# An mLSTM cell with its result laid out features-on-partitions: array halves and quarters, block transpose, shuffle, and a trip through memory

## Chip, cores, metric

One core of a Trainium2 chip. The metric is device time of one execution in microseconds (us), lower is better. A kernel's time is the median of its executions, which agree within 1%. "Granted clock" is the share of TensorE's full clock that the profile records as granted. Engines: PE is TensorE (PEld its weight load), DVE VectorE, ACT ScalarE, POOL GpSimd, SP SyncE, whose only work here is to issue DMAs, in order (in the changed kernel's queue below, the loads of xT at 383.03 us stand behind an output store that goes out at 381.40).

## The reference, cut to what matters

Batch 4, 8 heads, 768 tokens, head dimension 40; then a SwiGLU block, 320 to 1536 to 320, all fp32.

```
for t in range(S):                       # per batch and head
    m_new = max(f[t] + m, i[t])
    C = exp(f[t] + m - m_new) * C + exp(i[t] - m_new) * outer(v[t], k[t])
    n = exp(f[t] + m - m_new) * n + exp(i[t] - m_new) * k[t]
    y[t] = sigmoid(o[t]) * (C @ q[t]) / max(abs(n . q[t]), 1)
x = y as (tokens, heads * 40)
out = (silu(x @ w_gate) * (x @ w_val)) @ w_out
```

With these inputs n·q, computed by the reference, stays under 0.274 in size, so the clamp gives 1 throughout and the division changes nothing.

## The kernel before

The cell is computed in chunks of 128 tokens ("units"), six per batch element, 24 in all. Three units make a group of 384 tokens; there are eight groups. For each group PE first runs the *generator* (gate and value products over 12 slices of the 1536 features, with the next group's scores between them), then the *projection*, nine parts of 2.155 us, into which the cell of the next group is set. The next generator needs the next group's result, transposed, as `xT`. Each unit's weights `w` are made on DVE, POOL and ACT from a load of M, a running maximum of the gates that is computed at the start and kept in memory.

```
def attend(u):                                   # the cell of one unit
    inter[:, heads] = qT @ C                     # 4 full-array products
    y = inter * e_T                              # DVE
    add = k.T @ v_w;  new C = add + kept         # PE, POOL, DVE
    for h in range(H):                           # tokens on partitions: 41 streamed columns
        nc.tensor.matmul(intra[:, h, :], lhsT=un["w"][:, h, :], rhs=un["v"][:, h, :], start=True, stop=True)
    y = y + intra                                # DVE
    den = 1 / max(abs(y[:, :, D:]), 1)           # DVE, 8 elements per token
    x = o * y * den                              # POOL, DVE; x_sb has one buffer
    xx = x, each half doubled                    # POOL

def seam(u):                                     # features onto partitions, on PE
    for kc in range(NKC):
        nc.tensor.transpose(tp[:, kc, :], units[u]["x"][:, kc], ident)      # tp_x
    nc.scalar.copy(xts[g][...], tp)              # xT

# ... cut: order inside one projection of nine parts, n = -1 .. 8
follow = {-1: [(attend, nxt[0])], 1: [(attend, nxt[1])], 3: [(attend, nxt[2])],
          4: [(seam, nxt[0])], 5: [(seam, nxt[1])], 7: [(seam, nxt[2])]}
for n, u in zip((4, 5, 6), after):
    follow.setdefault(n, []).append((turn, u))   # k, q transposes of the group after
```

All DMAs are issued by SyncE. While the first group runs, DVE also converts the block's weights (`raw`) into their working form, 18 pieces.

Of the kernel before, what the change touches and what calls it, by code (L numbers as in the profile page):

```python
# [9 lines left out]
F32 = mybir.dt.float32  # L10
U32 = mybir.dt.uint32
AF = mybir.ActivationFunctionType
# [5 lines left out]
L = 128  # L18
# [4 lines left out]
def kernel(  # L23
# [22 lines left out]

    nc = tc.nc
# [5 lines left out]
    D1 = D + 1  # L53
# [7 lines left out]
    assert NB * L == S and NFC * 128 == DF and TW <= 512 and D <= DP and BH <= 128 and NKC * HP == DM  # L61
# [17 lines left out]
    NRK, NRQ, NRO = 2 * GC, GC + 1, GC + 1  # L79
    k_ring = [const.tile([128, H, DP], F32, name=f"k{r}") for r in range(NRK)]  # L80
    q_ring = [const.tile([128, H, DP], F32, name=f"q{r}") for r in range(NRQ)]
    v_ring = [const.tile([128, H, D1], F32, name=f"v{r}") for r in range(NRK)]
    for r in range(NRK):
        nc.vector.memset(k_ring[r][:, :, D:], 0.0)
        nc.gpsimd.memset(v_ring[r][:, :, D:], 1.0)
    for r in range(NRQ):
        nc.vector.memset(q_ring[r][:, :, D:], 0.0)

# [6 lines left out]
    def tokens(a, u):  # L95
        b, c = divmod(u, NB)
        return a[b, :, ts(c, L), :].rearrange("h p d -> p h d")

    def load(u):
        un = units[u] = {"k": k_ring[u % NRK], "q": q_ring[u % NRQ], "v": v_ring[u % NRK]}  # L100
        nc.sync.dma_start(out=un["k"][:, :, 0:D], in_=tokens(k, u))
        nc.sync.dma_start(out=un["q"][:, :, 0:D], in_=tokens(q, u))
        nc.sync.dma_start(out=un["v"][:, :, 0:D], in_=tokens(v, u))

    def load_o(u):
        un = units[u]
        un["o"] = work.tile([128, H, D], F32, name="o_sb", bufs=NRO)
        nc.sync.dma_start(out=un["o"], in_=tokens(o_gate, u))
        nc.scalar.activation(un["o"], un["o"], AF.Sigmoid)
# [14 lines left out]
    nc.vector.reduce_sum(pair, idb.rearrange("p (a two) -> p a two", two=2), axis=AX.X)  # L124
    half = const.tile([BH, 2], F32)
    nc.vector.reduce_sum(half, idb.rearrange("p (a two) -> p two a", two=2), axis=AX.X)
# [3 lines left out]
    C_ring = [const.tile([128, PR, 2, D1], F32, name=f"C{r}") for r in range(2)]  # L130
# [7 lines left out]
    def flat(t):  # L138
        return t.rearrange("p c t -> p (c t)")
# [10 lines left out]
    M_dram = tc.dram_tile([BH, S], F32, name="M_dram")  # L150
    nc.sync.dma_start(out=M_dram, in_=flat(M_sb))
# [4 lines left out]
    nc.scalar.activation(e_sb, e_sb, AF.Exp)  # L156


    g_T = const.tile([128, NB, BH], F32)
    e_T = const.tile([128, NB, BH], F32)  # L160
    for dst, src, c0 in ((g_T, g_sb, 0), (e_T, e_sb, 1)):
        tp = psum.tile([128, NB, BH], F32, name="tp_g", tag="cell")
        for c in range(c0, NB):
            nc.tensor.transpose(tp[:, c, :], src[:, c - c0, :], idb)
        nc.vector.tensor_copy(dst[:, c0:, :], tp[:, c0:, :])
# [55 lines left out]
    def weigh(u):  # L221

        b, c = divmod(u, NB)
        un = units[u]
        w = un["w"] = work.tile([128, H, L], F32, name="w_sb", bufs=2 * GC - 1)
        src = M_dram[b * H:(b + 1) * H, ts(c, L)].unsqueeze(0).to_broadcast([128, H, L])
        nc.sync.dma_start(out=w, in_=src)
        gb = g_T[:, c, b * H:(b + 1) * H].unsqueeze(2).to_broadcast([128, H, L])
        nc.vector.tensor_tensor(w, gb, w, op=ALU.subtract)  # L229
        nc.gpsimd.affine_select(w, w, compare_op=ALU.is_ge, fill=NEG, base=0, pattern=[[0, H], [1, L]],  # L230
                                channel_multiplier=-1)
        nc.scalar.activation(w, w, AF.Exp)  # L232
        if c + 1 < NB:
            un["v_w"] = work.tile([128, H, D1], F32, name="v_w", bufs=GC + 1)
            nc.gpsimd.tensor_tensor(un["v_w"], un["v"], w[:, :, L - 1:L].to_broadcast([128, H, D1]), op=ALU.mult)  # L235
# [10 lines left out]
    def scores(u):  # L246
        un = units[u]
        sps = [psum.tile([128, PR, L], F32, name="sp", tag="cell") for _ in range(2)]
        for j in range(PR):
            for two in range(2):  # L250
                r = slice(two * DP, two * DP + DP)
                nc.tensor.matmul(sps[two][:, j, :], lhsT=un["kT"][r, j, :], rhs=un["qT"][r, j, :], start=True, stop=True)  # L252
        w2 = un["w"].rearrange("p (j two) t -> p two j t", two=2)
        for two in range(2):
            nc.vector.tensor_tensor(w2[:, two], sps[two], w2[:, two], op=ALU.mult)  # L255

    def attend(u):
        b, c = divmod(u, NB)
        un = units[u]
        y = un["y"] = work.tile([128, H, D1], F32, name="y_sb")  # L260
        old = state.get("C")
        if c > 0:
            inter = psum.tile([128, H, D1], F32, name="inter", tag="cell")
            for j in range(PR):
                nc.tensor.matmul(inter[:, 2 * j:2 * j + 2, :].rearrange("p h d -> p (h d)"), lhsT=un["qT"][:, j, :],  # L265
                                 rhs=old[:, j].rearrange("p a d -> p (a d)"), start=True, stop=True)
            nc.vector.tensor_tensor(y, inter, e_T[:, c, b * H:(b + 1) * H].unsqueeze(2).to_broadcast([128, H, D1]),
                                    op=ALU.mult)
        if c + 1 < NB:
            add = psum.tile([128, PR, 2, D1], F32, name="add", tag="cell")  # L270
            for j in range(PR):
                nc.tensor.matmul(add[:, j].rearrange("p a d -> p (a d)"),  # L272
                                 lhsT=un["k"][:, 2 * j:2 * j + 2, :].rearrange("p h d -> p (h d)"),
                                 rhs=un["v_w"][:, 2 * j:2 * j + 2, :].rearrange("p h d -> p (h d)"),
                                 start=True, stop=True)
            new = C_ring[u % 2]
            if c > 0:
                d = dec[:, c - 1, b * PR:(b + 1) * PR].unsqueeze(2).unsqueeze(3).to_broadcast([128, PR, 2, D1])
                kept = work.tile([128, PR, 2, D1], F32, name="kept", bufs=1)
                nc.gpsimd.tensor_tensor(kept, old, d, op=ALU.mult)  # L280
            for two in range(2):
                r = slice(two * DP, two * DP + DP)
                if c > 0:
                    nc.vector.tensor_tensor(new[r, :, two], add[r, :, two], kept[r, :, two], op=ALU.add)  # L284
                else:
                    nc.vector.tensor_copy(new[r, :, two], add[r, :, two])
            state["C"] = new
        intra = psum.tile([128, H, D1], F32, name="intra", tag="cell")
        for h in range(H):
            nc.tensor.matmul(intra[:, h, :], lhsT=un["w"][:, h, :], rhs=un["v"][:, h, :],  # L290
                             start=True, stop=True)
        if c > 0:
            nc.vector.tensor_tensor(y, y, intra, op=ALU.add)  # L293
        else:
            nc.vector.tensor_copy(y, intra)
        den = work.tile([128, H, 1], F32, name="den")
        nc.vector.scalar_tensor_tensor(den, in0=y[:, :, D:], scalar=-1.0, in1=y[:, :, D:], op0=ALU.mult, op1=ALU.max)
        nc.vector.tensor_scalar(den, den, scalar1=1.0, scalar2=None, op0=ALU.max)
        nc.vector.reciprocal(den, den)
        x = work.tile([128, DM], F32, name="x_sb", bufs=1)  # L300
        x3 = x.rearrange("p (h d) -> p h d", d=D)
        nc.gpsimd.tensor_tensor(x3, un["o"], y[:, :, 0:D], op=ALU.mult)  # L302
        nc.vector.tensor_tensor(x3, x3, den.to_broadcast([128, H, D]), op=ALU.mult)
        xx = un["x"] = work.tile([128, NKC, 2, HP], F32, name="xx_sb", bufs=GC)
        nc.gpsimd.tensor_copy(xx, x.rearrange("p (c d) -> p c d", d=HP).unsqueeze(2).to_broadcast([128, NKC, 2, HP]))

    def seam(u):

        g, i = divmod(u, GC)
        if i == 0:  # L310
            xts[g] = work.tile([128, NKC, TW], F32, name="xT")
        for k0, k1 in ((0, PR), (PR, NKC)):
            tp = psum.tile([128, PR, L], F32, name="tp_x", tag="cell")
            for kc in range(k0, k1):
                nc.tensor.transpose(tp[:, kc - k0, :], units[u]["x"][:, kc].rearrange("p a d -> p (a d)"), ident)  # L315
            nc.scalar.copy(xts[g][:, k0:k1, ts(i, L)], tp[:, 0:k1 - k0, :])  # L316
        del units[u]
# [52 lines left out]
    for u in group(0):  # L370
        seam(u)
# [4 lines left out]
    for g in range(NG):  # L376
# [22 lines left out]
        if nxt:  # L399
            follow = {-1: [(attend, nxt[0])], 1: [(attend, nxt[1])], 3: [(attend, nxt[2])],  # L400
                      4: [(seam, nxt[0])], 5: [(seam, nxt[1])], 7: [(seam, nxt[2])]}
# [37 lines left out]
```

## Time and profile before

| | before |
|---|---|
| time, median of three runs | 701.59 us (699.84 to 702.41); 702.0 with the fourth run on record |
| profiled span | 699.5 us |
| end of the first generator stage | 155.2 us |
| a later group | 75.25 us: generator 41.65, projection with cell 33.6 |
| idle PE inside later groups | none |

From the page of the kernel before: an engine's busy time with its share of the span, and, second, the shares of the chain that ended last.

```profile
PE 644.2 (92%) x3909; PEld 457.6 (65%) x3909; DVE 324.7 (46%) x557; ACT 190.8 (27%) x317; POOL 130.9 (19%) x143
PE 81%; DVE 10%; issue 4%; ACT 2%; POOL 2%; DMA 2%; SPq 0%; DVEq 0%; POOLq 0%; ACTq 0%
```

The two agree: 92% busy and 81% of the chain say that PE is the bound; the DVE part of the chain lies in the start. The forty slices in the prediction show where. So only two things can pay here: less PE work in a group, or a shorter start.

### The profile page before, as it was taken

Reading aid. Unit: us, or ns where it says so; the run is one execution under the profiler, and the core shown is the slowest. Engines: PE = TensorE matmul, PEld = TensorE weight load, DVE = VectorE, ACT = ScalarE, POOL = GpSimd, SP = SyncE. Lnnn points to the kernel's source line nnn. Section 1 sums busy time; section 2 is a strip of 40 time slices with the busy share of each in tenths; the row PEclk is TensorE's granted clock in tenths of the full one; section 3 lists DMA queues with packets and bytes.
Section 4 is the critical chain, followed back from the end, with each engine's and each line's share of the span. In section 5 each row is a group of like instructions: output and inputs, shape, how many; then the busy total and the mean of one; then the engine's idle time right before and its main releaser. Section 6 shows DMA issues by size and latency. Waiting matters only on the chain.

```text
span 699.5 us, 9732 instructions
## 1 busy us (share of the span) xinstructions
PE 644.2 (92%) x3909; PEld 457.6 (65%) x3909; DVE 324.7 (46%) x557; ACT 190.8 (27%) x317; POOL 130.9 (19%) x143
## 2 busy tenths in 40 slices
PE   3578686579999999999999999999999999999998
PEld 3477453348766786678666876688667866686565
DVE  5688398995243533445134514443344324431330
ACT  3313533113511272115311461126112321101110
POOL 1355343333200330014000410032002200020000
PEclk9755797989999999999999999999999999999999
DMA  9969974325400460026100640044001100000000
GB/s 150 198 107 193 169 148 106 129 76 127 96 1 1 90 142 11 1 59 136 30 1 11 145 87 1 1 101 103 11 1 40 28 10 2 0 11 20 1 1 28
DMA packets 138141, 44.97 MB, mean 64 GB/s; under 512 B 101136, under 2 KB 136464, under 8 KB 138096
## 3 DMA queue, kind: packets, MB, share of 16 engines
q1 hardware_dynamic: 138096, 44.35, 31.4%
q8 instruction: 31, 0.51, 0.3%
q14 instruction: 14, 0.11, 0.1%
HBM read 40.30 MB, written 4.03 MB: 63 GB/s over the span
## 4 chain that ended last, share of the span: by engine, by line
PE 81%; DVE 10%; issue 4%; ACT 2%; POOL 2%; DMA 2%; SPq 0%; DVEq 0%; POOLq 0%; ACTq 0%
PE gv_ps L327 40%; PE o_ps L342 22%; PE intra L290 6%; PE add L272 3%; PE inter L265 3%; PE sp L252 2%; PE tp_kq L242 2%; PE tp_x L315 2%; DVE wgv_sb L199 1%; DVE size L205 1%; DMA raw<-in_moe_w_val_dram 1%; DVE raw L204 1%; POOL w_sb L230 1%; DVE wo_sb L199 1%; DVE wgv_sb L198 1%
## 5 line engine op out<-in xcount | busy, mean ns | idle before, releaser
L327 PE MATMUL gv_ps<-xT,wgv_sb 64*128 64x384 f32 x1920 | 334.9, 497 | 26.7 <-DVE sg L331 23.3
L327 PEld LDWEIGHTS gv_ps<-xT,wgv_sb 64*128 64x128 f32 x1920 | 194.3, 193 | 155.0 <-issue 22.7
L331 DVE TENSOR_TENSOR sg<-sg,gv_ps 128x384 f32<-128x384 f32 x96 | 53.0, 553 | 254.0 <-ACT sg L330 254.0
L342 PE MATMUL o_ps<-wo_sb,h_sb 128*128 128x320 f32 x576 | 165.0, 436 | 0.0
L342 PEld LDWEIGHTS o_ps<-wo_sb,h_sb 128*128 128x128 f32 x576 | 105.6, 190 | 38.4 <-issue 0.5
L330 ACT ACTIVATE sg<-gv_ps 128x384 f32<-128x384 f32 x96 | 46.9, 490 | 256.0 <-PE gv_ps L327 256.0
L333 DVE TENSOR_TENSOR h_sb<-sg,gv_ps 128x384 f32<-128x384 f32 x96 | 53.0, 553 | 9.0
L290 PE MATMUL intra<-v,w_sb 128*128 128x41 f32 x384 | 50.9, 297 | 1.2 <-issue 1.2
L290 PEld LDWEIGHTS intra<-v,w_sb 128*128 128x128 f32 x384 | 49.8, 210 | 1.4 <-issue 1.4
L235 POOL TENSOR_TENSOR v_w<-v,w_sb 128x328 f32<-128x328 f32 x20 | 16.0, 802 | 159.5 <-ACT sg L330 148.8
L280 POOL TENSOR_TENSOR kept<-C,dec 128x328 f32<-128x328 f32 x16 | 13.5, 845 | 166.2 <-DVE C L284 164.8
L229 DVE TENSOR_TENSOR w_sb<-g_T,w_sb 128x1024 f32<-128x1024 f32 x24 | 32.0, 1340 | 25.8 <-DMA w_sb<-M_dram 25.8
L230 POOL TENSOR_SCALAR_AFFINE_SELECT w_sb<-w_sb 128x1024 f32<-128x1024 f32 x24 | 29.1, 1216 | 45.2 <-DVE w_sb L229 36.3
L252 PEld LDWEIGHTS sp<-qT,kT 64*128 64x128 f32 x384 | 28.6, 205 | 12.0 <-DVE w_sb L255 6.6
L232 ACT ACTIVATE w_sb<-w_sb 128x1024 f32<-128x1024 f32 x24 | 25.4, 1057 | 40.6 <-POOL w_sb L230 40.4
L252 PE MATMUL sp<-qT,kT 64*128 64x128 f32 x384 | 29.6, 292 | 6.0 <-DVE w_sb L255 6.0
L255 DVE TENSOR_TENSOR w_sb<-sp,w_sb 128x512 f32<-128x512 f32 x48 | 31.2, 682 | 0.6 <-POOL v_w L235 0.6
L206 POOL TENSOR_TENSOR wgv_sb<-wgv_sb,size 128x640 f32<-128x640 f32 x12 | 20.9, 1739 | 45.1 <-DVE size L205 43.9
L302 POOL TENSOR_TENSOR x_sb<-o_sb,y_sb 128x320 f32<-128x320 f32 x24 | 21.9, 914 | 35.8 <-DVE y_sb L293 34.1
L316 ACT COPY xT<-tp_x 128x512 f32<-128x512 f32 (+1 forms) x48 | 18.2, 432 | 35.9 <-PE tp_x L315 35.9
L346 ACT COPY z_sb<-o_ps 128x320 f32<-128x320 f32 x24 | 10.3, 431 | 60.7 <-PE o_ps L342 33.8
L265 PEld LDWEIGHTS inter<-C,qT 128*128 128x128 f32 x160 | 22.2, 205 | 7.0 <-DVE C L284 2.6
(70 smaller groups left out, 464.7 us busy)
## 6 DMA issues: line engine op xcount, KB each, us to landing
w_sb<-M_dram SPq DMA_DIRECT2D x24, 512.0 KB, 5.2
k<-in_k_dram SPq DMA_DIRECT2D x24, 160.0 KB, 3.3
q<-in_q_dram SPq DMA_DIRECT2D x24, 160.0 KB, 3.5
v<-in_v_dram SPq DMA_DIRECT2D x24, 160.0 KB, 3.6
o_sb<-in_o_gate_dram SPq DMA_DIRECT2D x24, 160.0 KB, 3.5
raw<-in_moe_w_gate_dram SPq DMA_DIRECT2D x12, 320.0 KB, 4.2
raw<-in_moe_w_val_dram SPq DMA_DIRECT2D x12, 320.0 KB, 5.3
raw<-in_moe_w_out_dram SPq DMA_DIRECT2D x6, 640.0 KB, 3.9
```

Of the source, the lines that this page charges most:

```text
L229: nc.vector.tensor_tensor(w, gb, w, op=ALU.subtract)
L230: nc.gpsimd.affine_select(w, w, compare_op=ALU.is_ge, fill=NEG, base=0, pattern=[[0, H], [1, L]], channel_multiplier=-1)
L232: nc.scalar.activation(w, w, AF.Exp)
L252: nc.tensor.matmul(sps[two][:, j, :], lhsT=un["kT"][r, j, :], rhs=un["qT"][r, j, :], start=True, stop=True)
L255: nc.vector.tensor_tensor(w2[:, two], sps[two], w2[:, two], op=ALU.mult)
L265: nc.tensor.matmul(inter[:, 2 * j:2 * j + 2, :].rearrange("p h d -> p (h d)"), lhsT=un["qT"][:, j, :], rhs=old[:, j].rearrange("p a d -> p ...
L290: nc.tensor.matmul(intra[:, h, :], lhsT=un["w"][:, h, :], rhs=un["v"][:, h, :], start=True, stop=True)
L327: nc.tensor.matmul(ps[i], lhsT=wgv_sb[r, kc, ts(m, 128)], rhs=xts[g][r, kc, :], start=(kc == 0), stop=(kc == NKC - 1))
L330: nc.scalar.activation(sg, ps[0], AF.Sigmoid)
L331: nc.vector.tensor_tensor(sg, sg, ps[0], op=ALU.mult)
L333: nc.vector.tensor_tensor(h, sg, ps[1], op=ALU.mult)
L342: nc.tensor.matmul(p, lhsT=hs[g, m][:, ts(i, 128)], rhs=wo_sb[:, m, :], start=(m == 0), stop=(m == NFC - 1))
```

## The change

Intent: take PE's transposes of the result away. If a head's result comes out with features on the partitions in the first place, it is already what the generator wants, and the intra products load 64 columns of weights instead of 128, two of them side by side in the halves of the array. The price: the divisor now lies on one partition of each 32 and has to be spread by a shuffle, so the reciprocal runs over 512 elements per partition in place of 8; the output gate must be transposed too (32x32 blocks, on DVE); and because heads of 40 features do not stand where the generator's 64-row blocks want them, the result is packed through memory: stored in pieces and loaded back.

The core of the diff (cuts marked with "...."; the changed layout of q, k, v, C and of the decay, and the smaller number of buffers of xT and of the gate, are left out):

```diff
     def load(u):
-        nc.sync.dma_start(out=un["k"][:, :, 0:D], in_=tokens(k, u))
-        nc.sync.dma_start(out=un["q"][:, :, 0:D], in_=tokens(q, u))
-        nc.sync.dma_start(out=un["v"][:, :, 0:D], in_=tokens(v, u))
+        for a, name in ((k, "k"), (q, "q")):
+            for two in range(2):
+                dst = un[name].rearrange("p (j two) d -> p two j d", two=2)
+                nc.sync.dma_start(out=dst[:, two, :, 0:D], in_=tokens(a, u)[:, two * PR:(two + 1) * PR, :])
+        for c0, d0, d1 in parts:
+            nc.sync.dma_start(out=un["v"][:, :, c0:c0 + d1 - d0], in_=tokens(v, u)[:, :, d0:d1])
     def load_o(u):
....
+        for col in range(2):
+            for c0, d0, _ in parts:
....
+                nc.sync.dma_start(out=ob[col * HP + c0:col * HP + c0 + 32, :, 0:NSQ * D - d0], in_=src[:, :, d0:])
+        nc.scalar.activation(ob, ob, AF.Sigmoid)
+        nc.vector.transpose(oT...., ob....)
     def attend(u):
....
+                    onto(two * PR + j, old[r, j, :], un["qT"][r, j, :], False)     # inter, quarters
+        for h in range(H):
+            onto(h, un["v"][:, h, :], un["w"][:, h, :], True)                      # intra, column halves
....
+        x = work.tile([128, PR, L], F32, name="x_sb", bufs=1)
+        for two in range(2):
+            part = slice(two * PR // 2, (two + 1) * PR // 2)
+            nc.vector.stream_shuffle(r[:, part], ys[two], mask=[ONE] * 32)
+            nc.vector.tensor_tensor(x[:, part], ys[two], un["o"][:, part], op=ALU.mult)
+        nc.scalar.activation(r, r, AF.Abs)
+        nc.vector.tensor_scalar(r, r, scalar1=1.0, scalar2=None, op0=ALU.max)
+        nc.vector.reciprocal(r, r)
+        nc.vector.tensor_tensor(x, x, r, op=ALU.mult)
....
-            nc.scalar.copy(xts[g][:, k0:k1, ts(i, L)], tp[:, 0:k1 - k0, :])
+        xd = tc.dram_tile([PR, 2, D, L], F32, name=f"x_dram{u}")
+        for col in range(2):
+            for c0, d0, d1 in parts:
+                nc.sync.dma_start(out=xd[:, col, d0:d1]...., in_=x[col * HP + c0:col * HP + c0 + d1 - d0])
+        for half in range(2):
+            nc.sync.dma_start(out=xts[g][half * HP:(half + 1) * HP, :, ts(i, L)], in_=src)
-            follow = {-1: .... 4: [(seam, nxt[0])], 5: [(seam, nxt[1])], 7: [(seam, nxt[2])]}
+            follow = {-1: [(attend, nxt[0])], 1: [(attend, nxt[1])], 3: [(attend, nxt[2])]}
```

## The prediction

> **What bounds the kernel now.** I read the forty slices first. PE stands at 9 from about slice 9 on; before that PE is at 3 to 8 while DVE and DMA are near 9. So there are two regimes.
>
> ```profile
> PE   3578686579999999999999999999999999999998
> DVE  5688398995243533445134514443344324431330
> DMA  9969974325400460026100640044001100000000
> ```
>
> Next the view of windows, cut where the first generator stage ends (155.2 us), at group borders, and at 637.8, where the last generator stage begins:
>
> ```profile
> 82.00:155.20 73.20, 53.45 (x233) 32.00 (x233) 65.55 (x86) 18.36 (x27) 24.07 (x15) 0.82 0.53 126
> 188.90:230.48 41.58, 41.58 (x289) 25.84 (x289) 15.79 (x28) 5.83 (x12) 0.00 (x0) 1.00 0.01 5
> 305.73:339.40 33.67, 33.67 (x201) 27.50 (x201) 14.40 (x27) 15.92 (x25) 10.79 (x12) 1.00 0.51 111
> ```
>
> The columns after the stretch are its length and the busy time of PE, weight load, DVE, ACT and POOL, then clock, DMA share and GB/s. From 155.2 to 637.8 PE never stops: a group takes 75.25 us, 41.58 of generator matmuls with scores and 33.67 of projection with the next group's cell inside it. There only PE work counts. Before 155 us the generator stage takes 73.2 us instead of 41.6 because DVE (65.6 busy) converts weights.
>
> What the change touches on PE, from the chain of waits in order of time (start, length, what) and from the groups of instructions:
>
> ```profile
> 306.78 0.89 PE add L272 x8
> 307.67 1.75 PE intra L290 x16
> ```
> ```profile
> L290 PE MATMUL intra<-v,w_sb 128*128 128x41 f32 x384 | 50.9, 297 | 1.2 <-issue 1.2
> L290 PEld LDWEIGHTS intra<-v,w_sb 128*128 128x128 f32 x384 | 49.8, 210 | 1.4 <-issue 1.4
> L252 PE MATMUL sp<-qT,kT 64*128 64x128 f32 x384 | 29.6, 292 | 6.0 <-DVE w_sb L255 6.0
> ```
>
> An fp32 product appears as two instructions. Intra streams only 41 columns, yet 16 instructions take 1.75 us, 109 ns each, and weight load is busy just as long: it is bound by loading 128 columns of weights. The projection takes 2.155 us for 8 passes of 320 columns, 269 ns each, so a streamed column costs about 0.84 ns; 41 would be 35 ns. The scores, which use two row halves of the array, take 0.89 us for 8 heads of 128 columns.
>
> [...]the first inter after the row-half generator matmuls takes 1.05 us on the chain, against 0.87 for the later ones (313.64 to 314.50), 0.17 us for a switch. [...]The trace only has 8-element ones: 203 ns median and 184 at least, against 154 at least for a clamp of the same tile. [...]Here the output store lands after 1.8 us on the SyncE queue[...].
>
> **The change part by part.** On PE, per unit (128 tokens), at full clock:
> - Turn transposes (tp_x) go: 5 in 0.54 us (326.36 to 326.90).
> - Intra: 8 heads, each 64 weight columns and 128 streamed, alternating column halves. If column halves overlap as row halves do in the scores: 0.9 to 1.0 us instead of 1.75, so -0.8. Without overlap 16 passes of 109 ns are 1.75 us: nothing won.
> - Inter: 8 quarter-array products of 128 columns instead of 4 full ones. [...]I expect the scores' rate: 0.9 us against 0.87. Nothing won.
> - Add: 8 products of 64 weight columns, 48 streamed, four in a row on the same half[...], about 0.9 us against 0.89.
> - Mode changes: the cell was full-array inside a full-array projection. Now it goes full, quarters, halves, full: three switches at 0.15 (from the 0.17), +0.45 us.
>
> Sum: -0.54 -0.8 +0.45, so -0.87 us per unit. In the PE-bound part 21 units attend: -18 us. Rows busy in several engines' totals do not matter there; this is the number on the path.
>
> DVE, per unit. An elementwise op from PSUM costs about 155 ns plus 1.03 ns per element (0.50 us for 328 elements, 0.68 for 512). Removed: the two y ops 0.50 each, two C updates 0.33 each, three den ops 0.17 + 0.74 + 0.20, x by den 0.49: 3.3 us. Added: C 0.35 and a small copy 0.12; two shuffles and two products of 256 elements at 0.42, 1.7; the clamp 0.4; reciprocal of 512 elements; a product of 512, 0.68; and the block transpose of the gate, some 0.7. The reciprocal is my biggest guess: the 30 to 50 ns extra for 8 elements is 4 to 6 ns per element, so about 3.2 us. Sum 7.1 us, +3.8 per unit, some +90 us in all; without the slow reciprocal only +30. In a projection stage DVE goes from about 15 us of 33.7 to 26 of 31: still under PE, but no longer loosely so.
>
> POOL loses the o*y product and the doubling copy (0.81 + 0.72) and gains a product of 512 (about 1 us): no matter. ACT loses about 0.75 us of copies and gains Abs, about 0.6.
>
> DMA: v splits into 96 and 64 byte pieces, twice the packets; the broadcast of M gets 4 KB runs in place of 512 B; new are e (256 KB a unit), the result's 160 KB out and 320 KB back. Issues per unit go from 5 to 17; at 0.37 us each on the queue, 6.3 us a unit, 19 in a stage of 31. It fits.
>
> **The new path.** The next generator stage needs the last unit's result through memory. After the third attend stand five projection parts at 2.155 us and three k/q turns at 0.87: 13.4 us of cover (10.8 in the last such stage, which has no turns). The chain: two shuffles and products 1.7, Abs beyond them 0.7, clamp 0.4, reciprocal 3.2, product 0.7, so 6.7; DVE backlog from weights, transpose and the earlier attend 1 to 2; store 0.4 + 2.0, load 0.4 + 2.5 (k loads here land in 2.7). About 13 us against 13.4. I count 1 to 1.5 us exposed per group, seven groups: +8.
>
> Start: DVE is near its limit up to 68 us and from 82 to 155. Three cells at +3.1 and six transposes at 0.7 are +13 us there; some falls into the DVE hole before 81 us (8.7 us waiting for sg), and DMA, 97% busy from 27 to 82, gets about 20% more work. I count +11.
>
> Sum: 701.6 - 18 + 8 + 11 = 703, and a 1-in-4 chance that column halves do not overlap (worth 17 us) adds some 3: 706.
>
> **Rivals.**
> 1. Column halves overlap, the reciprocal runs at one element per cycle, the round trip is hidden: -18 and +4 at the start, 687. For it: 13.4 us of cover, and scores showing overlap of row halves. Against it: the 30 to 50 ns on an 8-element reciprocal.
> 2. The wait for tp_x is replaced by a wait for memory at each group's start: if SyncE, which issues in order, holds the result behind loads that wait for free buffers, 4 to 5 us per group, 725 to 730. For it: all the traffic of a group falls in this stage (DMA share 0.51), with stretches full. Against it: the queue issues just 3 to 4 DMAs per unit late in the stage.
> 3. DVE becomes the bound of the projection stage: if shuffle or transpose cost twice my figure, DVE's 26 us pass 31 and each group grows 3 to 5 us: 720 to 735.
> 4. No overlap of column halves: about 720.
>
> **Range and chances.** The gain is small and nearly fixed, the three costs vary by some 10 us each and mostly upward: 684 to 732 eight times in ten. Faster by over 2% (under 687.6) needs rival 1 entire: 0.17. Slower by over 2% (over 715.6) needs one of rivals 2 to 4: 0.33. Within: 0.5.
>
> **What will show it.** In the changed profile: intra at some 0.95 us on the chain (0.06 us per instruction); inter and add unchanged; a group's PE work 72 to 73 us; the 512-element reciprocal's mean at 3 us or at 0.7; an idle PE before the generator's first matmul, released by the DMA of xT, 0 to 2 us; the first generator stage ending 5 to 15 us after 155. Wrong would make me: 1.75 us for intra, a reciprocal at 0.7 us, or an xT wait over 4 us.

## The result, and the profile after

The changed kernel is correct and takes **762.56 us** (median of 4 runs, 760.34 to 763.75) against 702.0 us of the kernel before in the same rounds: a ratio of **1.086**, 95% interval 1.083 to 1.090. It is slower by 8.6%. Every ratio here is the mean time of one kernel's fast runs over that of the other's fast runs of the same rounds, so not quite the ratio of the medians quoted.

From the page of the changed kernel: busy shares, slices of PE, granted clock and DMA in tenths, and the chain that ended last.

```profile
PE 626.6 (82%) x4104; PEld 440.0 (58%) x4104; DVE 425.9 (56%) x659; ACT 193.0 (25%) x291; POOL 118.9 (16%) x129
...
PE   3244393668769998899969998999699999997998
...
PEclk9655596678889999899979998999899999998999
DMA  7775757655470046402640166007500220012000
...
PE 63%; DVE 11%; issue 11%; DMA 6%; POOL 3%; SPq 3%; ACT 2%; DVEq 0%; POOLq 0%; ACTq 0%
```

PE has less work than before (626.6 us against 644.2) in a longer span. Its row has holes now, a 6, 7 or 8 about once per group, the start is one and a half slices longer, and the clock row, which was 9 throughout once the start was over, has holes as well. PE's share of the chain fell from 81% to 63%; what came in is DMA, "issue" and SyncE.

Cutting both traces at the first and last matmul of each stage on PE's timeline gives where the 61.4 us between the two profiled spans (760.9 and 699.5) come from:

| part of the span | before | after | difference |
|---|---|---|---|
| to the end of the first generator stage | 155.2 | 183.9 | +28.7 |
| PE idle right before the seven later generator stages | -0.5 (overlap) | 32.9 | +33.4 |
| the seven later generator stages | 288.9 | 305.5 | +16.6 |
| eight projections, with the attend before each | 252.7 | 235.5 | -17.2 |
| after the last projection | 3.2 | 3.1 | -0.1 |

The idle times before the later stages are 7.53, 3.95, 7.27, 3.58, 6.60, 0 and 4.05 us.

**The saving is there.** PE's timeline of the changed kernel, one attend in the middle of the run (start, length, engine, line, operation, count; then the idle time before and what ended it):

```profile
351.90 0.67 PE L303 MATMUL yT<-qT,C 64*64 64x128 f32 x16
352.50 1.09 PE L303 MATMUL yT<-w_sb,v 128*64 128x128 f32 x16
353.42 0.89 PE L318 MATMUL add<-v_w,k 128*64 128x48 f32 x16
354.24 4.57 PE L378 MATMUL o_ps<-wo_sb,h_sb 128*128 128x320 f32 x16
```

From start to start: inter 0.60, intra 0.92, add 0.82, and the projection goes on at 354.24. The block is 2.34 us. Before it was 0.87 + 0.89 + 1.75 for inter, add and intra and 0.54 for the result's transposes, 4.05 us. Not all of the 1.71 us is won: the two projection parts behind the block take 4.51 us (from 354.24 to the next attend at 358.74 it is 4.50) where those of the kernel before take 4.39 (233.11 to 237.50).

**It is lost again at the seam.** The same kernel between the end of this group's last attend (367.28) and the next generator stage, first DVE, then SyncE's queue:

```profile
364.83 3.35 DVE L339 RECIPROCAL r_sb<-r_sb 128x512 f32<-128x512 f32 x1
...
370.00 1.19 DVE L133 STREAM_TRANSPOSE oT<-o 128x512 f32<-128x512 f32 x1
371.74 0.43 DVE L338 TENSOR_SCALAR r_sb<-r_sb 128x512 f32<-128x512 f32 x1 [0.55 <-ACT r_sb L337]
372.20 3.35 DVE L339 RECIPROCAL r_sb<-r_sb 128x512 f32<-128x512 f32 x1
375.47 1.16 DVE L257 TENSOR_TENSOR w_sb<-g_T,w_sb 128x1024 f32<-128x1024 f32 x1
376.55 0.74 DVE L336 TENSOR_TENSOR x_sb<-yT,oT 128x256 f32<-128x256 f32 x2
377.33 1.08 DVE L340 TENSOR_TENSOR x_sb<-x_sb,r_sb 128x512 f32<-128x512 f32 x1
```
```profile
378.43 1.55 SPq L348 DMA_DIRECT2D x_dram<-x_sb  x4
381.40 0.36 SPq L383 DMA_DIRECT2D out_dram<-z_sb  x1
...
382.29 0.56 SPq L255 DMA_DIRECT2D w_sb<-M_dram  x1
383.03 1.25 SPq L352 DMA_DIRECT2D xT<-x_dram  x2
384.32 4.79 SPq L130 DMA_DIRECT2D o<-in_o_gate_dram  x8
```

PE is done with the projection at 380.86: the cover is 13.6 us. The result's chain is 20.9. On DVE it takes 11.1 us. Read from start to start, 6.8 of them are this unit's own: two shuffles, the wait for Abs and the clamp, the reciprocal of 3.35, the products. The other 4.3 are work that stands before or between them: the rest of the reciprocal of the *unit before* (until 368.2, 0.8 us), that unit's two products (1.2, in the lines left out), a gate transpose (1.2) and the weights of a later unit (1.1). From x in place (378.4) to the first matmul (388.14) it takes 9.7: four store issues in 1.55; then 3.05 in which SyncE, in order, waits with an output store for the projection's end and issues loads of q and M; then the two load issues of xT, 1.25, done by 384.28; and 3.9 us until PE starts. The profile puts PE's wait down to "DMA o", which SyncE issues right behind xT; by time and need it is xT.

**And it costs clock.** Right after that gap, and for comparison a stage of the kernel before, on PE's timeline:

```profile
388.14 9.92 PE L363 MATMUL gv_ps<-xT,wgv_sb 64*128 64x384 f32 x39 [7.27 <-DMA o<-in_o_gate_dram]
```
```profile
339.33 6.72 PE L327 MATMUL gv_ps<-xT,wgv_sb 64*128 64x384 f32 x40
```

The same work, 39 or 40 instructions, takes 9.92 us instead of 6.72. The windows of three generator stages of the changed kernel (length, then PE, weight load, DVE, ACT, POOL busy; granted clock; DMA share; GB/s):

```profile
388.14:433.30 45.16, 45.16 (x290) 30.59 (x292) 16.41 (x29) 9.40 (x16) 3.64 (x3) 0.93 0.09 23
547.70:591.60 43.90, 43.89 (x290) 29.86 (x291) 16.23 (x29) 9.39 (x16) 3.64 (x3) 0.96 0.08 22
624.10:665.75 41.65, 41.65 (x293) 25.90 (x295) 15.79 (x28) 7.11 (x13) 3.83 (x3) 1.00 0.05 17
```

PE is busy all through all three. The stage behind a gap of 7.27 us is 45.16 long at clock 0.93, the one behind 6.60 us is 43.90 at 0.96, and the only one with no gap before it has the old 41.65 at 1.00. Length times clock gives 42.0, 42.1 and 41.65: nearly all of the 16.6 us in the table are clock. Three windows of a microsecond each behind the gap of 7.27 us show it (the clock is the third number from the end):

```profile
388.14:389.14 1.00, 1.00 (x3) 0.71 (x5) 0.64 (x1) 0.00 (x0) 0.23 (x1) 0.50 0.77 174
393.14:394.14 1.00, 1.00 (x5) 0.68 (x4) 0.00 (x0) 0.00 (x1) 0.00 (x0) 0.50 0.00 0
395.14:396.14 1.00, 1.00 (x9) 0.81 (x7) 0.72 (x2) 0.77 (x2) 0.00 (x0) 1.00 0.00 0
```

PE's clock is at half for some 6 us behind this gap (0.50 from 388.14 to 394.14) and back at 1.00 from 395.14, and all six gaps (3.58 to 7.53 us) are followed by a slower stage. The longest gap isn't the dearest, though: the stage behind 7.53 us lost 2.05 us, those behind 3.58 and 3.95 lost 2.83. In the runs below, all gaps of 2.33 to 2.91 us (in nr_w, nr_x, w_only_x6, o_pool and x_pool) were followed by stages at 0.92 to 0.96, 43.6 to 44.8 us long in place of 41.6 (in x_pool it is the last stage, 43.3 in place of 38.9), up to 0.6 us of it idle. Those of 0.5 to 1.85 us were followed by 1.00 and stages of 42.2 to 42.8 us (the last stage 39.5 to 39.6), but for one of m2_best: 1.16 us, with 0.26 more two matmuls later, and then this stage at 0.96:

```profile
273.40:317.88 44.48, 44.22 (x292) 28.13 (x295) 15.79 (x28) 7.73 (x15) 3.83 (x3) 0.96 0.22 50
```

### The profile page after: what moved, and what is told of

The parts are those of the page before. It is cut to its first block, busy times and chain, and to the rows that moved or that the text cites. A ratio compares the mean times of both kernels' runs of the same rounds, so it can differ in the third digit from the quotient of the medians.

```text
span 760.9 us, 10611 instructions
## 1 busy us (share of the span) xinstructions
PE 626.6 (82%) x4104; PEld 440.0 (58%) x4104; DVE 425.9 (56%) x659; ACT 193.0 (25%) x291; POOL 118.9 (16%) x129
## 4 chain that ended last, share of the span: by engine, by line
PE 63%; DVE 11%; issue 11%; DMA 6%; POOL 3%; SPq 3%; ACT 2%; DVEq 0%; POOLq 0%; ACTq 0%
PE gv_ps L363 38%; PE o_ps L378 16%; PE yT L303 3%; DVE r_sb L339 3%; PE tp_kq L270 2%; PE sp L281 2%; DMA w_sb<-M_dram 2%; PE add L318 1%; DMA raw<-in_moe_w_val_dram 1%; DMA o<-in_o_gate_dram 1%; DMA xT<-x_dram 1%; DVE wo_sb L228 1%; DVE size L234 1%; POOL wgv_sb L235 1%; DVE wgv_sb L231 1%
## 5 line engine op out<-in xcount | busy, mean ns | idle before, releaser
L363 PE MATMUL gv_ps<-xT,wgv_sb 64*128 64x384 f32 x1920 | 359.3, 517 | 69.6 <-DVE sg L367 27.8
L363 PEld LDWEIGHTS gv_ps<-xT,wgv_sb 64*128 64x128 f32 x1920 | 229.0, 201 | 186.5 <-issue 53.1
L339 DVE RECIPROCAL r_sb<-r_sb 128x512 f32<-128x512 f32 x24 | 80.3, 3344 | 0.6
L257 DVE TENSOR_TENSOR w_sb<-g_T,w_sb 128x1024 f32<-128x1024 f32 x24 | 30.7, 1280 | 48.9 <-DMA w_sb<-M_dram 48.9
L291 POOL TENSOR_TENSOR qT<-qT,e_bc 128x512 f32<-128x512 f32 x20 | 27.4, 1372 | 176.8 <-PE sp L281 176.8
L303 PE MATMUL yT<-w_sb,v 128*64 128x128 f32 x384 | 30.0, 304 | 10.9 <-DVE w_sb L284 10.9
L303 PEld LDWEIGHTS yT<-w_sb,v 128*64 128x64 f32 x384 | 23.2, 151 | 17.1 <-DVE w_sb L284 11.6
L318 PE MATMUL add<-v_w,k 128*64 128x48 f32 x320 | 20.5, 241 | 13.6 <-DVE x_sb L336 10.2
L133 DVE STREAM_TRANSPOSE oT<-o 128x512 f32<-128x512 f32 x24 | 26.4, 1114 | 8.9 <-ACT o L131 8.8
L337 ACT ACTIVATE r_sb<-r_sb 128x512 f32<-128x512 f32 x24 | 15.0, 627 | 55.3 <-DVE r_sb L335 55.3
L318 PEld LDWEIGHTS add<-v_w,k 128*64 128x64 f32 x320 | 19.6, 154 | 15.1 <-DVE x_sb L336 11.3
```

Of the source, the lines that this page charges most:

```text
L257: nc.vector.tensor_tensor(w, gb, w, op=ALU.subtract)
L303: nc.tensor.matmul(ys[two][col * HP:(col + 1) * HP, (h % PR) // 2, :], lhsT=lhsT, rhs=rhs, start=(two, col) in fresh, stop=last, skip_grou ...
L318: nc.tensor.matmul(add[two * DP:(two + 1) * DP, j], lhsT=un["k"][:, 2 * j + two, :], rhs=un["v_w"][:, h, :], start=(j == 0), stop=(j == PR ...
L339: nc.vector.reciprocal(r, r)
L363: nc.tensor.matmul(ps[i], lhsT=wgv_sb[r, kc, ts(m, 128)], rhs=xts[g][r, kc, :], start=(kc == 0), stop=(kc == NKC - 1))
```

## The experiments

Eighteen kernels, in the order of the questions. "Gaps" are PE's idle times right before the later generator stages.

### Is it the reciprocal, the dependence, or the queue?

**no_recip**: the changed kernel with the reciprocal left out (still correct, since the clamp gives 1).

```diff
-        nc.vector.reciprocal(r, r)
```

> The reciprocal is left out (the result is wrong on purpose: it is multiplied by the clamp instead of divided). Theory A, the Vector engine's chain sets when the result is ready: 3.35 us less on the last unit's chain and 3 to 4 us less of backlog from the unit before, so the idle PE before the generator stages (33 us in all in the changed kernel) and the slower clock after it (17 us) nearly go, and the start shortens by about 10 us: 690 to 705 us. Theory B, the round trip through memory behind other DMA issues sets it: the gaps shrink by less than half, 735 us or more.

Measured: 729.3 us, ratio to before 1.041 (1.038 to 1.044). All gaps are 0. But five stages are 47.5 to 48.4 us long. The groups of instructions of this run have the reason, and the same row of the changed kernel stands below it:

```profile
L257 DVE TENSOR_TENSOR w_sb<-g_T,w_sb 128x1024 f32<-128x1024 f32 x24 | 32.9, 1372 | 79.7 <-DMA w_sb<-M_dram 79.3
```
```profile
L257 DVE TENSOR_TENSOR w_sb<-g_T,w_sb 128x1024 f32<-128x1024 f32 x24 | 30.7, 1280 | 48.9 <-DMA w_sb<-M_dram 48.9
```

Without the reciprocal DVE waits 79.3 us for M in place of 48.9. M is now the late load: before the one that DVE waits for longest (13.2 us), SyncE issues other DMAs almost without pause from 360.0 to 368.5, and M lands at 373.2. DVE takes its next operations for the generator (sg at 374.33 and h_sb at 376.64) only behind the one that waited for M, and PE waits 1.06 and 1.39 us for them. PE idles 2.4 to 4.3 us in each of the five stages, and in four of them its granted clock is 0.93 to 0.96. The reciprocal's 33 us are real, and a second wait of some 30 us was hidden behind them.

**stale_x**: xT is loaded from the group before (wrong result), so it never waits for its own chain; everything else, the reciprocal too, stays.

```diff
-        src = xd.rearrange(....)
+        state["xd", u] = xd
+        src = state["xd", u - GC if g > 0 else u].rearrange(....)
```

> xT is loaded from the result of the group before (wrong on purpose), with the same stores, loads and bytes, so that the generator stage no longer waits for the newest result; group 0 unchanged. If the wait for the result (by whichever part) is what the steady stage loses, gaps and slow clock before groups 1 to 7 go: 33 + 17 us less, about 712 us, with the start as long as before (183 us). If the gap is DMA issue order alone and not the result, the gaps stay above 2 us each and the time above 740.

Measured: 730.57 us, ratio 1.042 (1.038 to 1.046). Gaps 0, stages 44.5 to 46.7. Taking the dependence away is worth as much as taking the reciprocal away. Both runs then meet a further limit, so the equal times alone do not prove it; that the gaps are 0 in both, and before_recip_w below, say that the reciprocal costs through its place on the path to xT.

**x_pool** (stores of x and loads of xT issued by GpSimd) and **o_pool** (the loads of the output gate issued by GpSimd):

```diff
-                nc.sync.dma_start(out=xd[:, col, d0:d1]....        # x_pool; the load of xT likewise
+                nc.gpsimd.dma_start(out=xd[:, col, d0:d1]....
-                nc.sync.dma_start(out=ob[....                      # o_pool
+                nc.gpsimd.dma_start(out=ob[....
```

> Stores of x and loads of xT are issued on the GpSimd queue instead of SyncE's; result right. Theory B (SyncE's in-order queue): the store goes out as soon as x is there and the load as soon as the store has landed, each gap falls by 3 us or more, and SyncE is 2.9 us per unit freer at the start: 725 to 740. Theory A (Vector chain): 755 to 762.

> Loads of the output gate (4 per unit) are issued on the GpSimd queue; result right. If the number of issues on SyncE's queue starves the weight conversion at the start (raw weights come only at 120 us), the first generator stage ends 8 us or more earlier than 183.9 and the total falls by 8 to 15 us; if transfers' bytes limit the start, it stays within 3 us.

Measured: 762.36 us (1.088) and 755.83 us (1.078). With x_pool the gaps are 7.15, 6.25, 7.33, 7.97, 7.54, 0.95 and 2.91; with o_pool much as in the changed kernel. o_pool's first generator stage ends at 185.5, not 8 us earlier as its test asked; its 6.7 us come from shorter projections (228.2 us in all against 235.5). SyncE's order alone is not the gap. In x_pool, at the same group, x is in place at 372.75 and PE starts at 380.94, 8.2 us in place of 9.7: 2.3 to issue the stores, 2.3 until they have landed, 1.3 to issue the load, 2.0 to the first matmul. A queue without SyncE's other issues saves 1.5 us there, and with DVE's part as long as it is that does not bring xT in time.

### What is the second wait?

Four versions without the reciprocal, with transfers on GpSimd's queue: **nr_x** (x and xT), **nr_w** (the loads of M), **nr_xoe** (x, xT, o and the decay e) and **w_only_x6**, whose label is a misnomer: it has x, xT *and* the loads of M there.

```diff
-        nc.vector.reciprocal(r, r)                                 # all four
-        nc.sync.dma_start(out=w, in_=M_dram[b][c]....              # nr_w, w_only_x6
+        nc.gpsimd.dma_start(out=w, in_=M_dram[b][c]....
```

> No reciprocal, and stores of x and loads of xT on the GpSimd queue (with these inputs the clamp gives 1, so the result still passes). Without the reciprocal alone it was 729 us. Theory C: SyncE's in-order queue, stopped at each store of x until x is there, sends the next group's k, q, v and M loads late. Then the first generator stage starts 8 us or more earlier than 87.2 us, its k and q turns no longer wait for q (15 us before), the later generator stages shrink from 47.5 to under 44 us: 695 to 708. If only the number of transfers counts, it stays at 725 to 732.

> No reciprocal, and only the broadcast loads of M (one per unit) on the GpSimd queue. If the 6 us that each generator stage still loses (47.5 instead of 41.6) come from Vector and Scalar work that waits in order behind a late M load, five stages lose it: about 29 us less than 729, near 700, with the start unchanged at 181 us. If the M loads are late because their buffers come free late, no change: 725 to 732.

> No reciprocal, and x, xT, the output gate and e all on the GpSimd queue, so that SyncE issues about as many transfers as in the kernel before. Theory C with the count of issues as part of it: start back to within 8 us of the kernel before (155 us), generator stages near 42 us, 680 to 695. If GpSimd's queue is as slow in order as SyncE's was, 715 or more.

> No reciprocal, with x, xT and the M loads on the GpSimd queue. Against the run with x and xT alone it tells whether M loads are held up by x on whichever queue carries both: in that case the generator stages lengthen again to 45 us or more, above 705 us; if not, 690 to 700.

Measured: nr_x 729.82 us (1.041), nr_w **706.84** us (1.006, 1.003 to 1.010), w_only_x6 713.35 us (1.017). nr_xoe's usual runs took 723.7 to 725.9 us (1.033); its profiled execution took 2144.89 us with PE 98% busy and the generator's matmuls at a mean of 1508 ns (517 in the changed kernel) at a recorded clock of 1.000. I have no explanation for that one execution and use nothing of its trace.

Moving the loads of M alone gives 22.5 us; the first generator stage still ends at 182.8 us, and later groups take 72 us on average. Where x is moved, gaps come back, 1.9 to 5.3 us before five stages (nr_x and w_only_x6). That GpSimd issues these DMAs between its own work (in o_pool its 96 issues take 53.3 us of its time, 561 ns each) is the likely reason; it was not tested. nr_x and nr_xoe, which leave M on SyncE, gain nothing or 4 us and refute the expectation that moving x clears the queue. So the second wait is M behind the other issues on SyncE, as no_recip's row says.

### Do more issues cost by themselves?

**before_split**: the kernel before with the loads of k, q, v in two issues each and that of o in four; same bytes.

```diff
-        nc.sync.dma_start(out=un["k"][:, :, 0:D], in_=tokens(k, u))
+        for hh in (slice(0, PR), slice(PR, H)):
+            nc.sync.dma_start(out=un["k"][:, hh, 0:D], in_=tokens(k, u)[:, hh])
....
```

> The kernel BEFORE the change, with each load of k, q and v issued as two halves and that of the output gate as four quarters: the same bytes and packets in 10 issues per unit instead of 4, nothing else. If the count of issues on SyncE's queue lengthens the start, the first generator stage ends 8 us or more later than 155.2 and the total grows by 8 to 20 us, with the steady groups at 75.25 us as before; if the start of the changed kernel is long for other reasons (Vector work, waits for x), it stays within 3 us of 701.

Measured: 702.23 us, ratio 1.001 (0.999 to 1.002). The expectation looked at the end of the first generator stage, and that moved the other way, to 147.0; but the projection behind it took 42.9 us in place of 33.7, so that both end 1.0 us later than before. In all, ten issues per unit in place of four cost nothing here; the changed kernel's 17 were not tried. That issues matter only where something urgent stands behind them fits with nr_w, but is not shown in general.

### Is DVE's extra work the loss, wherever it stands?

**before_recip**: the kernel before with two reciprocals of a 256-element scratch tile in each cell, 3.3 us of DVE per unit.

```diff
         nc.vector.reciprocal(den, den)
+        nc.vector.reciprocal(scr, scr)
+        nc.vector.reciprocal(scr, scr)
```

> The kernel before with two reciprocals of a 256-element scratch tile added on DVE in every cell, 3.3 us per unit and 80 us in all as in the changed kernel, result path unchanged (no memory round trip). If the changed kernel's loss is DVE work as such, groups after the first grow by several us each and the time goes to 730 or more. If it is the reciprocal's place in the path to xT through memory, the later groups stay at 75 us (the seam has some 8 us of cover), the start grows by at most three reciprocals, 10 us: 702 to 713.

Measured: 718.35 us, ratio 1.024 (1.022 to 1.025). This test missed its aim: nothing ties the scratch tile to a unit, so the scheduler put all 48 reciprocals into the first 250 us, where they lengthened the start by 1.9 us and the first group by some 15; the later groups, which had none, took 75.25 us. It says nothing on the question, and was repeated with a tie:

**before_recip_w**: the reciprocal is made in place on half of the unit's weights after their last use, so DVE takes it in each unit, between y and den.

```diff
         nc.vector.reciprocal(den, den)
+        nc.vector.reciprocal(un["w"][:, 0:PR], un["w"][:, 0:PR])
```

> The kernel before with one 512-element reciprocal in each cell (in place, on half of the weights tile after its last use), which DVE now takes between the last y and den, so in each unit and on the way to x. If DVE's extra 3.3 us per unit are the loss as such, or if any delay of x is, later groups grow by 3 to 5 us as in the changed kernel and the time passes 725. If the loss needs the short cover and the round trip through memory, the old path swallows it: from the last attend to its seam stand four projection parts, 8.6 us, so later groups stay at 75.3 us; only the start and the first group grow: 706 to 716.

Measured: 711.99 us, ratio 1.015 (1.012 to 1.018). The groups of instructions and the windows of one projection and the generator stage after it, in this run:

```profile
L300 DVE RECIPROCAL w_sb<-w_sb 128x512 f32<-128x512 f32 x24 | 80.4, 3348 | 2.6 <-PE intra L290 2.6
```
```profile
316.67:351.00 34.33, 34.10 (x201) 27.39 (x201) 22.75 (x30) 15.80 (x25) 11.83 (x12) 1.00 0.50 109
350.93:392.58 41.65, 41.65 (x290) 25.89 (x289) 15.79 (x28) 5.82 (x12) 0.00 (x0) 1.00 0.02 5
```

The same 80.4 us of reciprocals, on the old path: the projection takes 34.33 where it took 33.67, and the stage after it starts without a gap at full clock. No group loses more than 0.7 us. What it loses it loses in the start: the first generator stage ends at 165.8 instead of 155.2, +10.6. This is the cleanest separation: **in the steady part DVE's time as such cost next to nothing; what costs is its place on a path with too little cover.**

### What holds the projection up, and what the start?

**x_two**: the changed kernel with two buffers of x.

```diff
-        x = work.tile([128, PR, L], F32, name="x_sb", bufs=1)
+        x = work.tile([128, PR, L], F32, name="x_sb", bufs=2)
```

> The changed kernel with two buffers of x in place of one. If the single buffer holds up the three cells of the start (product waits for the store of the cell before), the first generator stage begins 5 to 10 us sooner and the time is 752 to 758; the gaps before later stages stay (cells are 4 us or more apart there). If the start is bound by DVE's work and the loads behind SyncE alone, nothing: 761.

Measured: 745.74 us, ratio 1.063 (1.061 to 1.065), 17 us faster than the changed kernel, but not where I expected it: the first generator stage begins at 90.28 as before. The projections became shorter, 223.6 us in all with their attends against 235.5, and the gaps too (24.7 us against 32.9), while the generator stages grew by 5 us. PE's waits before the add products, in the changed kernel and in this run:

```profile
L318 PE MATMUL add<-v_w,k 128*64 128x48 f32 x320 | 20.5, 241 | 13.6 <-DVE x_sb L336 10.2 <-DVE w_sb L284 3.4
```
```profile
L318 PE MATMUL add<-v_w,k 128*64 128x48 f32 x320 | 19.6, 236 | 3.4 <-DVE w_sb L284 3.4
```

The 10.2 us behind x_sb are gone. With one buffer, x of a unit cannot be written until the store of the unit before has landed; the product by the gate waits, with it the PSUM tile (PE's output buffer) that it reads, and so PE's next product. The prediction did not have this wait at all.

The start is read from one window each, from 0 to the end of the first generator stage (columns as above; the third number after the length is DVE's busy time): before, changed, before_recip_w, and m2_best of below.

```profile
0.00:155.23 155.23, 103.15 (x501) 76.04 (x501) 119.81 (x175) 49.28 (x72) 57.77 (x58) 0.77 0.78 144
```
```profile
0.00:183.89 183.89, 95.19 (x524) 66.61 (x527) 135.52 (x186) 53.42 (x70) 59.38 (x70) 0.72 0.65 143
```
```profile
0.00:165.81 165.81, 100.38 (x501) 71.84 (x501) 130.02 (x182) 54.68 (x76) 59.55 (x59) 0.75 0.74 134
```
```profile
0.00:172.74 172.74, 88.56 (x524) 63.78 (x527) 133.24 (x197) 56.29 (x71) 67.40 (x80) 0.77 0.78 155
```

DVE's work until then is 119.8, 135.5, 130.0 and 133.2 us, and what it idles 35.4, 48.4, 35.8 and 39.5. In before_recip_w 10.2 us more work made 10.6 us more start, one to one. In the changed kernel 15.7 us are work and 13.0 are idle time.

### A correct version with a short reciprocal

**tr_w**: in place of shuffle and wide reciprocal, the block transpose brings the divisor onto 16 columns per partition; clamp and reciprocal run on those; a second transpose, of a broadcast, spreads them. M's loads are on GpSimd's queue. **tr_w_raw** adds the raw weights on GpSimd's queue; **tr_w_rawact** has them on the Scalar engine's instead.

```diff
-            nc.vector.stream_shuffle(r[:, part], ys[two], mask=[ONE] * 32)
+            nc.vector.transpose(r[:, part], ys[two])
....
+        n = r.rearrange("p x (s f) -> p (x s) f", f=32)[:, :, ONE:ONE + 1]
+        nc.vector.scalar_tensor_tensor(den, in0=n, scalar=-1.0, in1=n, op0=ALU.mult, op1=ALU.max)
+        nc.vector.tensor_scalar(den, den, scalar1=1.0, scalar2=None, op0=ALU.max)
+        nc.vector.reciprocal(den, den)
+        nc.vector.transpose(r...., den.to_broadcast([128, PR * NSQ, 32]))
-            nc.sync.dma_start(out=raw[r]....           # tr_w_raw: gpsimd, tr_w_rawact: scalar
+            nc.scalar.dma_start(out=raw[r]....
```

> A right version: the reciprocal is taken of 16 columns after a 32x32 block transpose of the cell's result and spread back by a second block transpose (no shuffle, no Abs, no reciprocal of 512), and the M loads go out on the GpSimd queue. Without any reciprocal and with M on GpSimd it was 707. Transposes at 0.6, 0.6 and 1.1 us cost about 1.5 us per unit more than no reciprocal: 707 to 720, gaps before generator stages under 3 us; a gap of 7 us again would mean that the chain, not the reciprocal, is too long.

> As the version before, and the raw weight loads (30 in pairs) also on the GpSimd queue. If the start is long because raw weights wait on SyncE behind the next group's loads (they came at 115 us in the changed kernel), the first generator stage ends 10 us or more earlier than in the run without this: 690 to 705. If Vector work or x sets the start, no change.

> The same with the raw weight loads on the Scalar engine's queue. If the queue of issue is all that counts, as the run with GpSimd: 690 to 705; Scalar work delayed by issues and waits would show as a start that is longer again.

Measured: 703.24 us (1.003, 1.001 to 1.006), 699.02 us (0.996, 0.994 to 0.998) and 694.47 us (0.989, 0.986 to 0.991). The division done properly costs no more here than leaving it out (nr_w, 706.84). The first generator stage ends at 180.6, 179.2 and 173.4: the raw weights, which SyncE issued in order behind everything else of the start, were part of its idle time. Moving them to GpSimd's queue gave 1.4 us and to the Scalar engine's 7.2, so it also matters which queue takes them.

**m2_best** is tr_w_rawact with two buffers of x; **m2_best_st** has the stores of M and e on GpSimd's queue as well; **m3_start** is m2_best with x and xT of the first group alone on GpSimd's queue.

```diff
+        x = work.tile([128, PR, L], F32, name="x_sb", bufs=2)          # m2_best
+        nc.gpsimd.dma_start(out=M_dram[b]....                          # m2_best_st, e likewise
+        xq = nc.gpsimd if g == 0 else nc.sync                          # m3_start
```

> The fastest version so far (short reciprocal, M loads on GpSimd's queue, raw weights on the Scalar engine's) with two buffers of x. If the wait of x for its own store (4.1 us on DVE, 7.8 on PE's add) is what delays the start there, the first generator stage begins 4 to 9 us sooner and the time is 686 to 690. If DVE is behind it, 693 to 695.

> The same with the stores of M and e in the start on GpSimd's queue as well. If SyncE's order is still what holds the first broadcasts of M back, 2 to 5 us less than the run before it; otherwise the same within 1 us.

> The version with two buffers of x, with stores of x and loads of xT on GpSimd's queue for the first group alone. If the start waits for SyncE, in order, to go from store to landing to load three times (6.8 us a unit in that trace, the first store issued 5 us after x was ready), the first generator stage begins 4 to 8 us sooner and the time is 683 to 687. If GpSimd, busy with weights, holds them as long, 690 to 693.

Measured: m2_best **690.93** us, ratio 0.985 (0.983 to 0.987), correct, the fastest; m2_best_st 693.71 us (0.988), m3_start 694.90 us (0.991). m2_best lies just above its expected 686 to 690, and its generator begins only 2.2 us sooner than tr_w_rawact's (93.84), not 4 to 9. The last two are misses: the stores' order was not the cause, and in m3_start PE begins its first generator stage at 97.05, later than m2_best's 91.67. SyncE's three round trips of x were a plausible cause of the late start; GpSimd's queue does not cure it. Rows of m2_best's groups on DVE:

```profile
L335 DVE STREAM_TRANSPOSE r_sb<-yT 128x256 f32<-128x256 f32 x48 | 21.0, 437 | 8.1 <-PE yT L303 7.9
L343 DVE STREAM_TRANSPOSE rr_sb<-den 128x512 f32<-128x512 f32 x24 | 17.0, 710 | 0.8
L341 DVE RECIPROCAL den<-den 128x16 f32<-128x16 f32 x24 | 6.0, 251 | 1.0
```

The reciprocal went from 3344 ns to 251. The later groups of m2_best take 28.9 and 29.0 us for projection with cell, against 33.67 before: the saving of the new layout in full. Its start still ends 17.5 us later than the old one, 13.4 of it DVE work. That m2_best beats the kernel before is not all the layout's merit: raw weights on the Scalar engine's queue might help the kernel before too, which was not tried.

## Why the prediction was wrong

The prediction was 706 us (684 to 732); measured were 762.6. Step by step:

- **PE's saving: mechanism right, size too small.** I had -0.87 us per unit and -18 in all. The block fell by 1.71 us per unit: intra 0.92 and transposes -0.54 as forecast, but inter went from 0.87 to 0.60 where I expected no gain (16 passes in quarters in 0.60 us, against 0.89 for the scores' 16 passes of as many columns in halves), and of the three mode switches, for which I added 0.45 (an estimate from an inter of 1.05 us against 0.87 in the old trace), only some 0.12 us can be seen, in the projection parts behind the block (4.51 us against 4.39). The 0.9 for add was my estimate alone; it took 0.82. Per group 4.7 us, so -33 over seven, which m2_best has in full. The changed kernel keeps only -17.
- **"I count 1 to 1.5 us exposed per group, seven groups: +8": this step failed**, and it is the main one. It measured +33.4. The cover was right (13.6 us against my 13.4). The chain was 20.9 instead of 13. On DVE it took 11.1 in place of 8 to 9: the unit's own work was right (6.8 against 6.7, with a reciprocal of 3.34 for a guessed 3.2), but the backlog, put at 1 to 2, was 4.3: the unit before is still on DVE, and a gate transpose and a later unit's weights come between. Through memory it took 9.7 in place of 5.3: store issues 1.55 instead of 0.4, 3.05 of waiting and other issues between store and load, 1.25 for the load's issues, and 3.9 to the start. (The 2.0 us for the store to land was an estimate; the old trace had 1.8 for the output store.) no_recip and stale_x, which cut the chain at different places, both make all gaps 0; before_recip_w shows that the same DVE work elsewhere does not make them. (The terms as printed add to 13 to 14 us, not 13, and the PE terms to -0.89, not -0.87; a quarter of 17 is 4, not 3. None of this matters.)
- **No step had the clock.** An idle PE was priced at its idle time. Each of the six gaps cost 2.0 to 3.5 us more in the stage behind it: +16.6 in all.
- **"17 issues per unit ... It fits" failed as an argument.** The sum fits, the order does not: M's loads come late, which the gaps hid and no_recip laid open (729.3, where taking gaps and lost clock out of the span would have left about 711: 761 less 33 less 17); moving M alone gave 22.5 us (nr_w). before_split shows that ten issues a unit by themselves cost nothing.
- **The single buffer of x was not looked at.** x_two took 11.9 us off the projections and 8 off the gaps. The diff shows `bufs=1` under a store that now has to land first; I did not ask when that buffer comes free.
- **Start: "+11 (DVE +13)" against +28.7.** DVE's part was near (+15.7). The other 13.0 are waits: in tr_w, a later version with the same layout, moving the raw weights off SyncE's queue took 7 us off (180.6 to 173.4, tr_w_rawact), so a like part of the 13.0 is probably theirs; in the changed kernel itself this was not run. The rest is open.
- **The rivals.** Rival 1 needed the round trip hidden and a reciprocal at one element per cycle, which was its assumption and not shown: 512 elements took 3.34 us. Rival 2 (the result held behind other transfers in SyncE's order, 4 to 5 us per group) came near in size but not in cause: x_pool moved it off that queue and gained nothing (1.5 us of 9.7 at the gap that was read). Rival 3, DVE as the bound of the projection stage, is refuted: from the end of one generator stage to the next DVE is busy 25.8 us of 36.2 (351.97 to 388.14), near the forecast 26, and before_recip_w adds 3.3 us a unit with a loss of at most 0.7 us a group. Rival 4 is refuted by the 0.92 us of intra.
- **The warning was there.** I wrote that an xT wait over 4 us would make me wrong, and that all three costs vary "mostly upward", and still let the range end at 732. Two costs that grow together out of one chain (gap and clock) do not average out.

Still open: what makes the start of m2_best 17.5 us longer than before beyond DVE's 13.4 us of work, and why w_only_x6, with x, xT and M on GpSimd's queue, ends its first generator stage at 170.9 where nr_w, with M alone there, ends at 182.8; why single gaps differ (3.6 to 7.5) and what sets the loss of clock behind each; and the one execution of 2144.89 us.

## What to carry to other kernels

When a result's hand-over moves from an engine to memory, write its chain down issue by issue, with what the in-order engines have in front of it at that time (the unit before, other loads), and hold it against the cover; sums of busy time do not show it. Price an idle TensorE with the clock that it loses behind the gap: here 2.0 to 3.5 us behind each gap of the changed kernel, and behind gaps of 2.33 to 2.91 us in other runs the stages were still at least 2.0 us longer. When one wait is removed, look at once for the one that it hid, and when a buffer's reader becomes a DMA, give it a second buffer.

## What was measured of the hardware

- Reciprocal on DVE: 3344 ns for 512 fp32 elements per partition (changed kernel), 251 for 16 (m2_best); by estimate from these two about 6.2 ns per element ((3344 - 251) / 496). In the changed kernel a transpose of 512 elements took 1.1 us and a product of as many 0.73.
- Transpose on DVE: 710 ns for 512 elements from a broadcast, about the time of a product of as many in the same run (m2_best, 689 ns); the output gate's transpose of as many elements, which writes with a stride of four elements, took 1114 ns in the changed kernel. The stride as the cause was not tested.
- Mode switches of PE: three per attend left some 0.12 us that can be seen, 4.51 us against 4.39 for the two projection parts behind the block.
- PE's clock: 0.50 for some 6 us behind a gap of 7.27 us; gaps of 2.33 to 2.91 us in five runs, and one of 1.16 and 0.26 in m2_best, were followed by stages at 0.92 to 0.96.
- The way through memory, from x in place to PE's first use of it: 9.7 us on SyncE's queue with other issues between, and 8.2 on GpSimd's queue (x_pool).
